# Summing the ninth chunk's first x earlier and centring it later, and moving one set of PE transposes behind eight products, in a fused linear-attention and MLP kernel

## The chip, the cores and the metric

The kernel runs on one core of one Trainium2 chip. The metric is the device time of one execution in microseconds. The engines are named as in the profile: PE (TensorE; its weight loads are PEld), DVE (VectorE, "Vector" in the text), ACT (ScalarE, "Scalar"), POOL (GpSimd) and SP (SyncE, which here only issues DMAs). Inputs are float32; the kernel computes in bfloat16 with float32 accumulation and writes float32.

## The reference

Shapes: batch B = 8, heads H = 8, sequence S = 576, head dimension D = 64, so the model width DM is 512 and the hidden width 2048.

```python
q_s = softmax(q, axis=-1)                  # over the 64 entries of a head
k_s = softmax(k, axis=2)                   # over the sequence
kv  = einsum('bhsd,bhse->bhde', k_s, v)
x   = einsum('bhsd,bhde->bhse', q_s, kv)   # then heads side by side: (B, S, 512)
xn  = (x - mean(x)) / sqrt(var(x) + 1e-6) * g_ln
out = x + relu(xn @ w_ch1) @ w_ch2
```

## The kernel before, in words

**Chunks.** The rows are worked in nine chunks of 512 rows, four tiles of 128. Chunks 1 to 8 (`c` = 0 to 7 in the code) hold the first 512 rows of each batch. The ninth (`C9` = 8) holds the 64 rows that are left of each of the eight batches. While PE runs the MLP of one chunk, the attention part of the next one is done between its matmuls; during chunk 8 this is the ninth chunk's.

**A tile's way to the MLP.** `po_mm` (L377) multiplies the exponentials of q with the batch's `kv` into a PSUM tile `po`; there are two such PSUM banks. `x_fast` (L410) does two Vector operations: L413 scales `po` by the reciprocals of q's sums (`rq`), writes x and sums it over the row by an accumulator (a second short instruction, DVE_READ_ACCUMULATOR, writes the sum into `mv`), and `xn_out` (L402, operation L405) writes `xn` = 512 x - sum, that is the centred x. `square_sum` (L395, Scalar) sums the squares of the centred x for the variance. `xn` is then transposed to `xnT`, two tiles at a time by a transposing DMA on SP (`xn_T`, L260), or, for batch 1's four tiles at the end of chunk 1, by PE: `xn_pT` (L918) calls `pe_T` (L895), four transposes into a PSUM tile `ptr` (L898) and a copy out of it, for tiles 0 and 1 by Scalar (L900).

**The MLP.** From chunk 3 on the first layer (`mm1_fast`, L718), and from chunk 2 on the second (`mm2_fast`, L649), use seven products in place of eight. In the first layer the hidden columns go in two halves, each of seven products in the order 1, 5, 6, 2, 7, 3, 4, each product of 2 groups x 4 matmuls of 256 columns. Products 1, 6, 7 and 4 accumulate onto one another in the same PSUM banks `bx` (one for each group), and between them Scalar and Vector take what they need: after product 1 a Scalar copy (`bc`), after 5 a Scalar copy (`s`), after 6 a Vector add into `bb` (L746), after 7 a Vector add that makes a quarter of `hT` (`out_22`, L749). Product 4 writes over what L749 reads, so it waits for it, group by group. Every second group's quarter then gets its relu on Vector (L754). `hs` are sums of blocks of `hT` (`sum_h`, L543), for the second layer's products.

**The order of the work** is written out by hand. `run` (L811) goes through the chunk's matmuls, each with a weight, and ahead of the matmul at which the sum of weights reaches a side task's position it issues that task. An engine's instructions run in the order of their issue. In chunk 8 a first-layer matmul counts 0.5: the second half begins at 28, product 6 ends at 40, product 7 at 48, product 4 at 56, and the second layer begins there. In chunk 1 the second layer (`mm2_stream`, L508, matmuls `pc` of 512 columns) counts 1 a matmul and goes from 64 to 128; batch 1's work at its end is in the list at L1094 to L1120.

The side tasks of chunk 8 are in `attn_rest` (L881): the ninth chunk's q sums (steps 1 and 27) and their reciprocal (28), `po` of tiles 0 and 1 (14) and of tiles 2 and 3 (58), `x_fast` at 40.5, 54, 66 and 75, `square_sum`, and the transposing DMAs at 61 and 78. `sum_h` has two more positions in chunk 8: 30 and 41.

`att_ps` has two PSUM banks (`po`, and the products `pkv` of k and v), `mm_ps` six for all else; which of the six a tile gets follows from the order in which tiles are released.

Of the kernel before, what the change touches and what calls it, by code (L numbers as in the profile page):

```python
# [20 lines left out]
def kernel(  # L21
# [16 lines left out]
    nc = tc.nc  # L38
# [14 lines left out]
    C9 = B  # L53
# [43 lines left out]
    def load_w2(k0, kn=4):  # L97
        rows = slice(k0, k0 + kn)
        nc.gpsimd.dma_start(w2_sb[:, rows, :], w2_src[:, rows, :])
# [105 lines left out]
    def reduce_q(c, t, tn=1):  # L205
        ts = slice(t, t + tn)
        nc.vector.reduce_sum(eqs[c][1][:, ts], eqs[c][0][:, ts], axis=AX.X)  # L207
# [25 lines left out]
    def sum_x(c, i):  # L233

        if i == 0:
            tqs[c] = mlp.tile([P, 4, 2, 2, P], BF16, tag="tq", name="tq", bufs=1)
        (b11, b12), (b21, b22) = [
            [xnTs[c][:, 2 * half : 2 * half + 2, 2 * kh : 2 * kh + 2, :] for half in range(2)]
            for kh in range(2)
        ]  # L240
        t1, t2, t3, t4 = [tqs[c][:, n] for n in range(4)]
        dst, x, y = ((t1, b12, b11), (t2, b22, t1), (t3, b22, b12), (t4, b21, t2))[i]
        eng = nc.vector if c >= C9 - 1 else nc.gpsimd
        for t in range(2):
            eng.tensor_tensor(out=dst[:, t], in0=x[:, t], in1=y[:, t], op=ALU.subtract)  # L245
# [6 lines left out]
    def dma_T(dst, src, t0, tn):  # L252
        nc.sync.dma_start_transpose(
            dst[:, t0 : t0 + tn].rearrange("p t j c -> p (t j) c"), src
        )
# [4 lines left out]
    def xn_T(c, t0, tn):  # L260
        dma_T(xnTs[c], xs[c][2][:, t0 : t0 + tn].rearrange("p t n -> p (t n)"), t0, tn)
# [104 lines left out]
    def start_x(c):  # L366
        xs[c] = (
            mlp.tile([P, T, DM], BF16, tag="x", name="x"),
            mlp.tile([P, T, 6], FP32, tag="st", name="st"),
            mlp.tile([P, T, DM], BF16, tag="xn", name="xn", bufs=1),  # L370
            mlp.tile([P, T, 2], FP32, tag="mv", name="mv"),
        )
        xnTs[c] = mlp.tile([P, T, KO1, P], BF16, tag="xnT", name="xnT")
# [21 lines left out]
    def square_sum(c, t):  # L395
        x, _, _, mv = xs[c]
        nc.scalar.activation(  # L397
            scrap, x[:, t], AF.Square, bias=mv[:, t, 0:1], scale=-float(DM),
            accum_out=mv[:, t, 1:2],
        )  # L400

    def xn_out(c, t, cols=slice(0, 512)):  # L402

        x, _, xn, mv = xs[c]
        nc.vector.tensor_scalar(  # L405
            out=xn[:, t, cols], in0=x[:, t, cols], scalar1=float(DM), scalar2=mv[:, t, 0:1],
            op0=ALU.mult, op1=ALU.subtract,
        )

    def x_fast(c, t):  # L410

        x, _, _, mv = xs[c]
        nc.vector.scalar_tensor_tensor(  # L413
            x[:, t].rearrange("p (h d) -> p h d", h=H),
            in0=pobox[c, t].rearrange("p (h d) -> p h d", h=H), scalar=1.0,
            in1=eqs[c][2][:, t].to_broadcast([P, H, D]), op0=ALU.mult, op1=ALU.mult,
            accum_out=mv[:, t, 0:1],
        )
        xn_out(c, t)

    def x_plain(t):

# [3 lines left out]
    def rstd_op(c):  # L426
        mv = xs[c][3]
        lnv = sml.tile([P, T], FP32, tag="lnv", name="lnv")
        rstds[c] = mlp.tile([P, T], FP32, tag="rstd", name="rstd")
        nc.scalar.activation(  # L430
            lnv, mv[:, :, 1], AF.Ln, bias=eps_ln, scale=1.0 / DM ** 3
        )
        nc.scalar.activation(rstds[c], lnv, AF.Exp, scale=-0.5)
# [373 lines left out]
    def spread(fns, a, b):  # L807
        n = len(fns)
        return [(a + (b - a) * i / n, fn) for i, fn in enumerate(fns)]
# [29 lines left out]
    def recip_q(c):  # L839
        nc.vector.reciprocal(eqs[c][2], eqs[c][1])  # L840
# [40 lines left out]
    def attn_rest():  # L881

        s = [(1, lambda: reduce_q(C9, 0, 2)), (27, lambda: reduce_q(C9, 2, 2)), (28, lambda: recip_q(C9)), (4, lambda: start_x(C9))]
        for t, (p0, p1, p2) in enumerate(((14, 40.5, 48), (14, 54, 62), (58, 66, 69), (58, 75, 77))):
            s += [(p0, lambda t=t: [po_mm(C9, t, i) for i in range(NP)])]
            s += [(p1, lambda t=t: x_fast(C9, t)), (p2, lambda t=t: square_sum(C9, t))]
        s += [(61, lambda: xn_T(C9, 0, 2)), (78, lambda: xn_T(C9, 2, 2)), (88, lambda: rstd_op(C9))]
        return s + spread([lambda i=i: sum_x(C9, i) for i in range(4)], 102, 104)

    def norm_q(b, t):  # L890
# [24 lines left out]
    def eq_pT(c, t, eng):  # L915
        pe_T(eqTs[c], eqs[c][0][:, t].rearrange("p h d -> p (h d)"), t, eng)

    def xn_pT(c, t, eng):  # L918
        pe_T(xnTs[c], xs[c][2][:, t], t, eng, None if c else g_col)
# [154 lines left out]
    with tc.manual_schedule(  # L1074
        engines={mybir.EngineType.PE, mybir.EngineType.DVE, mybir.EngineType.Activation,
                 mybir.EngineType.SP, mybir.EngineType.Pool}
    ):
        first_batch()
        load_behind(1, (2, 0))
        load_w2(8)  # L1080
        load_behind(1, (1,))
        load_w2(12, 2)
        load_w2(14, 2)
        load_behind(2)

        def po_x(c, t):
            for i in range(NP):
                po_mm(c, t, i)
            x_fast(c, t)

        run(
            mlp_steps(0),
            [
                (4, lambda: (eq_pT(0, 3, nc.scalar), x_plain(0), q0_rest(2), x_fast(0, 2))),  # L1094
                (8, lambda: (q0_rest(3), x_fast(0, 3))),
                (8.5, lambda: x_plain(1)),
                (10, lambda: xn_pT(0, 2, nc.vector)),
                (14.5, lambda: xn_pT(0, 3, nc.vector)),
                (22, lambda: square_sum(0, 0)),
                (26, lambda: square_sum(0, 1)),  # L1100
                (30, lambda: square_sum(0, 2)),
                (34, lambda: square_sum(0, 3)),
                (38, lambda: rstd_op(0)),
            ]
            + [(70, lambda: exp_q(1, 0, 4)), (72, lambda: exp_q(1, 2, 4))]
            + [(75 + t, lambda t=t: reduce_q(1, t)) for t in range(T)]
            + [((82, 86, 94, 98)[t], lambda t=t: eq_pT(1, t, nc.scalar)) for t in range(T)]
            + [(84, lambda: nc.vector.reciprocal(eqs[1][2], eqs[1][1]))]
            + [(88, lambda: exp_k(1, 0, 4)), (92, lambda: exp_k(1, 2, 4))]
            + [(26 + 4 * i, lambda i=i: scale_w1(i % KO1, i // KO1)) for i in range(2 * KO1)]  # L1110
            + [(p, lambda i=i: quarter_w2(i, 0)) for i, p in enumerate((60, 62, 64, 66))]
            + [(p, lambda i=i: sum_w1(i, 0)) for i, p in enumerate((80, 84, 88, 92))]
            + [(p, lambda i=i: sum_w1(i, 1)) for i, p in enumerate((96, 98))]
            + [(103 + 0.4 * j, lambda j=j: cast_v(1, j)) for j in range(2)]
            + [(104.5, lambda: prep_kvrem(1))]
            + [(111, lambda: (kv_all(1), start_x(1)))]
            + [(117, lambda: (po_x(1, 0), po_x(1, 1)))]
            + [(121.5, lambda: xn_pT(1, 0, nc.scalar)), (125, lambda: square_sum(1, 0))]
            + [(124.1, lambda: (po_x(1, 2), po_x(1, 3)))]
            + [(124, lambda: xn_pT(1, 1, nc.scalar)), (127, lambda: square_sum(1, 1))]  # L1120
        )
        for c in range(1, B):
            side = []
            if c == 1:
                side += second_side()
            else:
                if c + 1 < B:
                    side += attn_fast(c + 1)
                else:
                    side += attn_rest()  # L1130
                    side += [(6 + i, lambda i=i: sum_x(c, i)) for i in (2, 3)]
                if c + 2 < B:
                    side += [(1, lambda b=c + 2: load_batch(b))]
                    side += [(26, lambda b=c + 2: load_v(b))]
                    side += prep_fast(c + 2)
            if c == B - 2:
                side += [(1, load_qrem)]
                side += spread([lambda r=r: exp_qrem(r) for r in range(T)], 58, 80)
                side += [(84, lambda: eq_T(C9))]
            sums = [(57, 0)] if c == FAST else [(p, i) for i, p in enumerate((30, 41))]  # L1140
            run(mlp_steps(c), side + [(at, lambda i=i: sum_h(0, i)) for at, i in sums])
        run(mlp_steps(C9), [(33 + 3 * i, lambda i=i: sum_h(0, i)) for i in range(2)])
# [30 lines left out]
```

## Time and profile before

| what | value |
|---|---|
| median of 3 runs | 265.0 us (264.79 to 265.59) |
| profiled execution | 265.22 us |
| its span, first to last instruction | 263.0 us |
| PE busy | 257.0 us of the span (98%) |
| DVE, ACT, POOL busy | 216.8, 181.2, 77.2 us |
| granted TensorE clock | 1.00 |

A row of the instructions in order of time gives start, length, engine, line and operation, what is written from what, the count, and in brackets how long the engine had been idle and what ended this. Where a row holds several instructions ("x8"), its length goes from the first one's start to the last one's end. PE's matmuls overlap: the next one starts before the end of the one ahead of it is reached, so their pace is read from start to start. A row of the waits gives engine and line, the engine and line waited for, the total, the number of times and the longest.

### The profile page before, as it was taken

To read this page: it belongs to the slowest core of one execution; us is meant where nothing else is said; L and a number is where in the kernel's file an instruction comes from. 1 tells how busy PE (TensorE), PEld (TensorE's weight loads), DVE (VectorE), ACT (ScalarE), POOL (GpSimd) and SP (SyncE) were. 2 spreads that over 40 slices of the span, in tenths; PEclk is the share of its full clock that TensorE was granted. 3 is DMA by queue.
4 is the path that set the end of the run, shared out by engine and by line. 5 is a ranking of instruction groups with operands and counts; after the bars stand their busy time and mean duration, and the time that the engine had idled before them with its cause. 6 is when DMAs were issued, how large, how long until landed. Compare 5 with 4: busy or idle time off the path is not lost.

```text
span 263.0 us, 6811 instructions
## 1 busy us (share of the span) xinstructions
PE 257.0 (98%) x2700; PEld 218.1 (83%) x2700; DVE 216.8 (82%) x480; ACT 181.2 (69%) x356; POOL 77.2 (29%) x128
## 2 busy tenths in 40 slices
PE   8999999999999999999999999999999999999993
PEld 5799755766888998899889989998898887888883
DVE  5657686988989997899789978997899889977873
ACT  4688671997966788678867886788777477438400
POOL 8751226303067008500850095009100300030000
PEclk9999999999999999999999999999999999999999
DMA  6999999979967994899489969997807610422014
GB/s 220 258 201 206 339 213 311 277 157 287 177 125 219 300 157 81 248 285 142 79 275 277 127 76 280 266 129 152 248 3 95 188 44 0 82 87 75 0 42 120
DMA packets 69879, 45.00 MB, mean 171 GB/s; under 512 B 41492, under 2 KB 66072, under 8 KB 69848
## 3 DMA queue, kind: packets, MB, share of 16 engines
q0 software_dynamic: 20352, 22.29, 39.1%
q1 hardware_dynamic: 48896, 21.76, 38.4%
q10 hardware_dynamic: 600, 0.53, 0.6%
q8 instruction: 21, 0.34, 0.6%
q14 instruction: 10, 0.08, 0.1%
HBM read 36.70 MB, written 9.44 MB: 175 GB/s over the span
## 4 chain that ended last, share of the span: by engine, by line
PE 94%; DVE 3%; ACT 1%; issue 0%; ACTq 0%
PE ba L563 21%; PE bx L715 17%; PE bb L715 8%; PE ph L466 8%; PE bb L563 5%; PE be L563 5%; PE bc L563 5%; PE pc L512 5%; PE bc L715 5%; PE warm L829 3%; PE ph L451 3%; PE po L383 2%; PE pkv L347 2%; PE ptr L898 1%; PE xt L320 1%; DVE x L413 1%
## 5 line engine op out<-in xcount | busy, mean ns | idle before, releaser
L563 PEld LDWEIGHTS <-hs 128*128 128x128 bf16 x512 | 49.6, 98 | 5.6
L715 PEld LDWEIGHTS <-w_q 128*128 128x128 bf16 x448 | 43.2, 98 | 4.9
L563 PEld LDWEIGHTS <-hT 128*128 128x128 bf16 x392 | 37.3, 98 | 4.4
L715 PEld LDWEIGHTS <-w1g 128*128 128x128 bf16 x336 | 32.2, 98 | 4.9 <-issue 1.0
L245 POOL TENSOR_TENSOR tq<-xnT 128x256 bf16<-128x256 bf16 x20 | 12.9, 661 | 79.1 <-DMA xnT<-xn 46.7
L563 PE MATMUL ba<-w_q,hs 128*128 128x256 bf16 x256 | 31.7, 273 | 0.0
L580 POOL DMA_DIRECT2D out_dram<-ot x28 | 15.3, 555 | 47.0 <-DVE ot L574 47.0
L715 PE MATMUL bx<-tq,w_q 128*128 128x256 bf16 x224 | 29.0, 273 | 0.0
L397 ACT ACTIVATE scrap<-x,mv 128x512 bf16<-128x512 bf16 x36 | 25.9, 720 | 1.7 <-DVE x L413 1.3
L413 DVE SCALAR_TENSOR_TENSOR x<-po,rq 128x512 bf16<-128x512 f32 x34 | 23.3, 685 | 1.4 <-PE po L383 1.2
L739 ACT COPY bc<-bx 128x512 f32<-128x512 f32 x28 | 15.2, 593 | 13.0 <-PE bx L715 13.0
L746 DVE TENSOR_TENSOR bb<-bx,s 128x512 f32<-128x512 f32 x28 | 18.2, 694 | 7.1 <-ACT s L743 7.1
L757 ACT ACTIVATE hT<-bc 128x512 bf16<-128x512 f32 x28 | 15.3, 594 | 12.2 <-PE bc L715 12.2
L543 DVE TENSOR_TENSOR hs<-hT 128x1024 bf16<-128x1024 bf16 x32 | 20.9, 674 | 0.9 <-ACT hT L757 0.5
L207 DVE TENSOR_REDUCE zq<-eq 128x16 f32<-128x1024 bf16 (+1 forms) x20 | 20.8, 1051 | 1.0 <-ACT eq L190 0.8
L757 ACT ACTIVATE hT<-bb 128x512 bf16<-128x512 f32 x28 | 15.2, 594 | 8.2 <-PE bb L715 8.2
L749 DVE TENSOR_TENSOR hT<-bx,s 128x512 bf16<-128x512 f32 x28 | 18.0, 684 | 2.8 <-PE bx L715 2.8
L383 PE MATMUL po<-kv_sb,eqT 128*128 128x128 bf16 x120 | 20.2, 219 | 0.0
L588 ACT COPY s<-ba 128x512 f32<-128x512 f32 x15 | 8.7, 579 | 12.0 <-PE ba L563 7.3
L563 PE MATMUL ba<-w_sb,hT 128*128 128x256 bf16 x128 | 16.7, 273 | 0.0
L563 PE MATMUL bb<-w_q,hs 128*128 128x256 bf16 x128 | 16.5, 273 | 0.0
L757 ACT ACTIVATE hT<-bx 128x512 bf16<-128x512 f32 x28 | 15.4, 603 | 0.5 <-PE bx L715 0.5
(146 smaller groups left out, 539.3 us busy)
## 6 DMA issues: line engine op xcount, KB each, us to landing
out_dram<-ot POOLq DMA_DIRECT2D x32, 256.0 KB, 5.9
qt<-in_q_dram SPq DMA_DIRECT2D x5, 1024.0 KB, 7.2
kt<-in_k_dram SPq DMA_DIRECT2D x5, 1024.0 KB, 14.6
vt<-in_v_dram POOLq DMA_DIRECT2D x7, 512.0 KB, 14.0
qt<-in_q_dram POOLq DMA_DIRECT2D x2, 1024.0 KB, 12.6
kt<-in_k_dram POOLq DMA_DIRECT2D x2, 1024.0 KB, 13.4
w_sb<-in_moe_w_ch_dram POOLq DMA_DIRECT2D x3, 512.0 KB, 15.9
kt<-in_k_dram SPq DMA_DIRECT2D x4, 288.0 KB, 4.7
```

The source lines that it names most:

```text
L207: nc.vector.reduce_sum(eqs[c][1][:, ts], eqs[c][0][:, ts], axis=AX.X)
L383: nc.tensor.matmul(pobox["p"][:, i * P : i * P + P], eqTs[c][:, t, i, :], kv_sb[:, c, i, :], start=True, stop=True,)
L397: nc.scalar.activation(scrap, x[:, t], AF.Square, bias=mv[:, t, 0:1], scale=-float(DM), accum_out=mv[:, t, 1:2],)
L413: nc.vector.scalar_tensor_tensor(x[:, t].rearrange("p (h d) -> p h d", h=H), in0=pobox[c, t].rearrange("p (h d) -> p h d", h=H), scalar=1. ...
L466: nc.tensor.matmul(ph[:, m % 2, at : at + tn], (w1g if c else w1_sb)[:, ko, m * P : (m + 1) * P], xnTs[c][:, t0 : t0 + tn, ko, :], start=( ...
L543: nc.vector.tensor_tensor(out=dst, in0=x, in1=y, op=op)
L563: nc.tensor.matmul(dst, lhsT, rhs, start=first and (own or t == 0) and k == 0, stop=k == KH - 1, skip_group_check=True)
L580: nc.gpsimd.dma_start(out[c, 0:SM, :].rearrange("(p t) n -> p t n", t=T)[:, t], ybox[c, t])
L715: nc.tensor.matmul(dst[:, q], lhsT, rhs, start=first and q == 0 and ko == 0, stop=ko == 1, skip_group_check=True)
L746: nc.vector.tensor_tensor(out=at[g, "b"], in0=at[g, "x"], in1=at[g, "s"], op=ALU.add)
L749: nc.vector.tensor_tensor(out=h_out(g, 1, 1), in0=at[g, "x"], in1=at[g, "s"], op=ALU.add)
L757: nc.scalar.activation(h_out(g, odd, half), at[g, name], AF.Relu)
```

## The change

Two things. The ninth chunk's first tile: its L413 is issued at step 31 of chunk 8 instead of 40.5, without its `xn_out`, which is issued at 54.5, behind the second tile's `x_fast` (54); its `square_sum` moves from 48 to 46, which changes nothing in Scalar's order. And in chunk 1, `xn_pT` of batch 1's tile 1 moves from position 124 to 124.5, behind the products and x of tiles 2 and 3 (124.1). No operation is added or removed.

On Vector, the first x goes from behind the two `bb` adds of chunk 8's second half to ahead of them, and the first `xn` from there to behind the second tile's `xn`. On PE, the four transposes of tile 1 go behind one `pc` and the eight `po` matmuls of tiles 2 and 3. Since tiles are then allocated in another order, the next twelve or so tiles in `mm_ps` get other banks; from then on each tile follows the same predecessor as before. The queues of Scalar, GpSimd and SP keep their order.

```diff
-    def x_fast(c, t):
+    def x_fast(c, t, centre=True):
...
-        xn_out(c, t)
+        if centre:
+            xn_out(c, t)
...
     def attn_rest():
...
-        for t, (p0, p1, p2) in enumerate(((14, 40.5, 48), (14, 54, 62), (58, 66, 69), (58, 75, 77))):
+        for t, (p0, p1, p2) in enumerate(((14, 31, 46), (14, 54, 62), (58, 66, 69), (58, 75, 77))):
             s += [(p0, lambda t=t: [po_mm(C9, t, i) for i in range(NP)])]
-            s += [(p1, lambda t=t: x_fast(C9, t)), (p2, lambda t=t: square_sum(C9, t))]
+            s += [(p1, lambda t=t: x_fast(C9, t, t > 0)), (p2, lambda t=t: square_sum(C9, t))]
         s += [(61, lambda: xn_T(C9, 0, 2)), (78, lambda: xn_T(C9, 2, 2)), (88, lambda: rstd_op(C9))]
+        s += [(54.5, lambda: xn_out(C9, 0))]
...
             + [(117, lambda: (po_x(1, 0), po_x(1, 1)))]
             + [(121.5, lambda: xn_pT(1, 0, nc.scalar)), (125, lambda: square_sum(1, 0))]
             + [(124.1, lambda: (po_x(1, 2), po_x(1, 3)))]
-            + [(124, lambda: xn_pT(1, 1, nc.scalar)), (127, lambda: square_sum(1, 1))]
+            + [(124.5, lambda: xn_pT(1, 1, nc.scalar)), (127, lambda: square_sum(1, 1))]
```

## The prediction, made before the result was known

> **What bounds the kernel now.** I read the page first, then who waits for whom on PE, then the instructions in order of time around the two places that the change touches.
>
> ```profile
> span 263.0 us, 6811 instructions
> ...
> PE 94%; DVE 3%; ACT 1%; issue 0%; ACTq 0%
> ```
>
> ```profile
> PE bx L715 <- DVE hT L749: 0.6, 1, 0.6
> PE ptr L898 <- DVE xn L405: 0.2, 1, 0.2
> ```
>
> The first two rows are the page's: the chain that ended last runs over PE for 94% of the span, so a microsecond counts only where PE stands still. The other two are PE's waits, apart from one in the program's first microseconds, and they are the change's two places: `bx` products wait for Vector's `hT`, and transposes (`ptr`) for Vector's `xn`. Both waits are longer than their rows, because a matmul's modelled end reaches past the moment at which the next could start. I therefore count from start to start.
>
> The first place is the second half of chunk 8's first layer, Vector and then PE in order of time:
>
> ```profile
> 215.44 0.63 DVE L543 TENSOR_TENSOR hs<-hT 128x1024 bf16<-128x1024 bf16 x1
> 216.71 1.30 DVE L746 TENSOR_TENSOR bb<-bx,s 128x512 f32<-128x512 f32 x2 [0.64 <-ACT s L743]
> 217.92 0.68 DVE L413 SCALAR_TENSOR_TENSOR x<-po,rq 128x512 bf16<-128x512 f32 x1
> 218.52 0.08 DVE L413 DVE_READ_ACCUMULATOR x<-po,rq 128x1 f32 x1
> 218.64 0.35 DVE L405 TENSOR_SCALAR xn<-x,mv 128x512 bf16<-128x512 bf16 x1
> 218.91 0.69 DVE L543 TENSOR_TENSOR hs<-hs,hT 128x1024 bf16<-128x1024 bf16 x1
> 219.51 1.28 DVE L749 TENSOR_TENSOR hT<-bx,s 128x512 bf16<-128x512 f32 x2
> ...
> 221.17 0.68 DVE L413 SCALAR_TENSOR_TENSOR x<-po,rq 128x512 bf16<-128x512 f32 x1
> ...
> 222.17 0.68 DVE L543 TENSOR_TENSOR hs<-hT 128x1024 bf16<-128x1024 bf16 x1
> ```
>
> ```profile
> 216.86 1.04 PE L715 MATMUL bc<-xnT,w1g 128*128 128x256 bf16 x8
> 217.74 1.04 PE L715 MATMUL bx<-tq,w_q 128*128 128x256 bf16 x8
> 218.61 1.04 PE L715 MATMUL bb<-xnT,w_q 128*128 128x256 bf16 x8
> 220.25 1.19 PE L715 MATMUL bx<-tq,w1g 128*128 128x256 bf16 x8 [0.60 <-DVE hT L749]
> 221.28 0.60 PE L563 MATMUL ba<-w_sb,hT 128*128 128x256 bf16 x4
> 221.81 0.64 PE L390 MATMUL po<-kv_sb,eqT 128*64 128x128 bf16 x16
> 222.38 1.48 PE L563 MATMUL ba<-w_sb,hT 128*128 128x256 bf16 x12
> 223.70 0.49 PE L563 MATMUL bb<-w_q,hs 128*128 128x256 bf16 x3
> ```
>
> Eight of these matmuls take 0.87 us from start to start (216.86, 217.74, 218.61). The last `bx` products were thus due at 219.48 and came at 220.25, 0.77 late; `ba` was due another 0.87 later, at 221.12, and came at 221.28, so 0.16 more went between the two groups of four. **PE lost 0.93 us here.** The cause is Vector's order: it waits idle for 0.64 ahead of the `bb` adds, and then from 216.71 it has no gap: two adds, the sum of x (0.72 until `xn` starts), the centring `xn` (0.27 until the next start), `hs`, and only then the two `hT` adds whose sources PE is to overwrite.
>
> The second place is the end of the first chunk, PE and one row of Vector:
>
> ```profile
> 45.77 0.59 PE L512 MATMUL pc<-w_sb,hT 128*128 128x512 bf16 x2
> 46.54 0.40 PE L898 MATMUL ptr<-ident,xn 128*128 128x128 bf16 x4 [0.17 <-DVE xn L405]
> 46.77 0.38 PE L512 MATMUL pc<-w_sb,hT 128*128 128x512 bf16 x1
> 46.99 0.61 PE L383 MATMUL po<-kv_sb,eqT 128*128 128x128 bf16 x8
> 47.43 0.81 PE L512 MATMUL pc<-w_sb,hT 128*128 128x512 bf16 x3
> 48.08 1.91 PE L466 MATMUL ph<-xnT,w1g 128*128 128x256 bf16 x16
> ```
>
> ```profile
> 46.13 0.35 DVE L405 TENSOR_SCALAR xn<-x,mv 128x512 bf16<-128x512 bf16 x1
> ```
>
> A 512-column `pc` takes 0.22 from start to start (46.77 to 46.99). Two from 45.77 end at 46.21; the transposes start at 46.54, when `xn` (end 46.48) is there. **PE lost 0.33 us here.**
>
> **The change part by part.** *The ninth chunk's first x.* No operation is added or removed: L413 with its accumulator read moves ahead of the two `bb` adds, and its L405 goes behind the second tile's L405, so behind `hT`. Its inputs are old by then: the first two tiles' products ran some 5 us earlier (step 14), and the reciprocal at step 28 stands ahead of `hs` in Vector's queue. `hs` hands over 0.60 after its start (218.91 to 219.51), so x starts at 215.44 + 0.60 = 216.04. It holds Vector 0.72, as it does now until `xn` starts, so the adds start at 216.76 instead of 216.71: x fits into the idle 0.64 but for 0.05. From the adds' start the next operation comes 1.21 later (216.71 to 217.92), and it is now `hs`; 0.60 on, at 218.57, `hT` starts instead of at 219.51.
>
> Now PE. The first `bx` came 0.74 after `hT`'s start (219.51 to 220.25): that is 219.31, and PE is due at 219.48: no wait. The second four need the second `hT`, whose pair ends 1.28 after its start, 219.85, plus the same hand-over of 0.06 (first `hT` ends some 0.69 after 219.51, PE at 220.25): 219.91. They are due at 219.48 + 0.44 = 219.92: just in time. One wait upstream becomes tighter: the `bx` products of 217.74 accumulate onto what the adds read, and their second four (218.18) need the second add, 216.76 + 1.30 + 0.06 = 218.12: 0.06 to spare. So the 0.93 goes whole, or with up to 0.05 left if the accumulator read hands over more slowly to an add than to `xn`. I take **0.92**.
>
> The Trainium skill's page "VectorE: DVE Perf Modes", section "The DRAIN you can't avoid", speaks for a larger remainder: the next operation does not start until the pipe is empty. By it x and its read would hold Vector 0.68 + 0.08 = 0.76, the second `hT` would reach PE 0.03 too late, and the sum below would be 1.03 instead of 1.06. The trace has the pair of adds in 1.30, less than 2 x 0.69, so a start comes a little ahead of the previous end; I keep 0.72.
>
> What is late next: the delayed `xn` is hidden by what stands behind the second x. The second x now starts about 221.17 - 0.94 = 220.23 and frees its PSUM bank at 220.95; the fourth tile's products need that bank in the second half of the `po` block, which moves from 221.81 to 220.88, so at about 221.08: free in time by 0.13. Vector then does two centrings (0.27 more) and is at `hs` at 221.50 instead of 222.17. Vector is thus ahead by 0.67, PE by 0.93; the difference of 0.26 must be covered by slack downstream:
>
> ```profile
> 229.14 0.88 DVE L574 SCALAR_TENSOR_TENSOR ot<-bc,rstd,x 128x256 f32<-128x256 f32 x2 [0.43 <-PE bc L563]
> 229.94 0.49 DVE L245 TENSOR_TENSOR tq<-xnT 128x256 bf16<-128x256 bf16 x2
> ```
>
> The `hs` of 222.17 feeds the second eight `bb` matmuls, due 223.70 + 0.87 - 0.93 = 223.64, while it ends at 222.18. At 229.14 Vector has stood idle for 0.43, waiting for PE: that covers the 0.26. The sync queue's transposing DMAs wait for the centrings of two tiles each; the first pair is now done in the other order but 0.67 earlier, the second pair 0.67 earlier too. What they bring is read at 229.94, where Vector itself would be up to 0.26 more ahead: a short wait may arise there, on Vector alone, since these sums are for the next chunk's products.
>
> *Batch 1's tile 1.* The four transposes go behind one `pc` and the eight `po`. PE then runs on from 46.21: `pc` to 46.42, `po` to 46.87 (0.45, 46.99 to 47.43), the transposes at once, since `xn` has been there since 46.54. The bank for the second `po` tile is free: its x was summed before `xn` started at 46.13. The three `pc` end at 46.87 + 0.22 + 0.65 = 47.74, so 0.34 earlier than 48.08. But `ph` needs Scalar's copy of these transposes:
>
> ```profile
> 46.97 0.59 ACT L900 COPY xnT<-ptr 128x512 bf16<-128x512 bf16 x1 [0.41 <-PE ptr L898]
> ...
> 49.97 1.06 ACT L477 ACTIVATE hT<-ph 128x512 bf16<-128x512 f32 x2
> 50.92 0.58 ACT L900 COPY xnT<-ptr 128x512 bf16<-128x512 bf16 x1
> ```
>
> It started 0.43 after the transposes (46.54 to 46.97), so now at 47.30, and ends at 47.89: PE can go on at about 47.92. **Of 0.33, 0.16 remains**; the rest has become a wait for the copy.
>
> Behind that copy Scalar is full. Busy PE, PEld, DVE, ACT and POOL of two stretches:
>
> ```profile
> 47.00:56.00 9.00, 9.00 (x87) 7.68 (x86) 8.56 (x17) 8.97 (x16) 2.22 (x4) 1.00 1.20 246
> 56.00:62.00 6.00, 6.00 (x69) 3.05 (x68) 4.59 (x13) 4.98 (x12) 2.36 (x4) 1.00 0.60 175
> ```
>
> Scalar works 8.97 of 9.00 us and has gaps only in the second stretch. So all its work in between comes 0.33 later while PE comes 0.16 earlier, and each place where PE waits for Scalar loses 0.49 of slack. Two are tight. Behind 48.08 come 24 `ph` (0.109 each) and two sets of transposes (0.22 each), up to 51.15; in the changed program the next `ph` takes the PSUM bank that the first relu (49.97, half of 1.06) frees. That relu now ends at 50.88, and PE is there at 50.99. Eight `ph` later, at 52.02 before and 51.86 now, the first layer turns to tiles 2 and 3 and needs the copy of 50.92: it will end at 51.83 and be seen at 51.88. So 0.14 is left. After this the banks come free about a microsecond ahead of need, and Scalar's gaps take up the delay. I take **0.14**, with 0.33 as the end that no copy would limit and a loss of 0.33, Scalar's whole delay, as the other.
>
> The sum is 0.92 + 0.14 = 1.06. PE runs to the end with no other wait, so the end moves by it. The profiled execution took 265.22 us with a span of 263.0, so 2.2 lie around it: 264.16, span 261.9. That run is 0.22 above the median of 265.0; on the median's scale the forecast is **263.9**.
>
> **The rivals.** *Batch 1 gives nothing:* Scalar's delay eats the 0.14. For it: the copy's margin at 52.02 is zero. Against it: at 52.02 the copy would have to come later still. With the 0.92 alone: 264.1.
>
> *The idle time isn't usable:* x holds up the adds by its whole 0.72. Then the second `bx` four of 218.18 wait 0.61, the rest follows, and only the centring's 0.3 is gained; with batch 1's part 264.6. Against it: nothing that x reads is younger than the `hs` of 215.44.
>
> *A wait in place of the one removed (slower):* Vector starts its operations in the order of the program, as all its rows do, so if x starts at s, the adds follow at s + 0.72, and PE loses s - 216.10 at `bx` plus some 0.05 at the second `hT`. This passes the present 0.93 at s = 216.98; each 0.1 us beyond costs 0.1. It would need a late release of x's operands or of its buffer, which the seventh chunk's outputs last read. They end here:
>
> ```profile
> 207.66 0.88 DVE L574 SCALAR_TENSOR_TENSOR ot<-ba,rstd,x 128x256 f32<-128x256 f32 x2
> ```
>
> That is 208.5, far ahead. A start two microseconds late, at 218.04, without batch 1's part, gives 265.0 + 1.06 = 266.1.
>
> **How the numbers follow.** Forecast 263.9: 0.66. Batch 1 nothing, 264.1: 0.16. Idle time not usable, 264.6: 0.11. Slower, 266.1 or so: 0.07. The range reaches from 265.0 - 0.93 - 0.33 with 0.2 for the spread of a median (the three runs lie 0.8 apart), 263.5, to the third case with the same 0.2, 264.8. About 0.3%, 0.8 us, is what a measurement of this kernel can tell from no change. The forecast clears it by only 0.26, so I give a sixth of its chance and a third of the first rival's to "within": faster 0.55 + 0.11 = 0.66; within 0.28; slower by more than that 0.06.
>
> **What would show it.** The x sum at about 215.9 (all times from here about 0.15 earlier than in the rows above), the adds with hardly any idle time ahead of them, no PE wait on `hT`, chunk 8 shorter by 0.9; at the first chunk's end no wait on `xn`, a short PE wait on the copy ahead of `ph`, and the Scalar copy at 47.3. A PE wait on `bb` L746, or on Scalar between 48 and 60, would prove me wrong.

## The result, and the profile after

| | before | changed |
|---|---|---|
| median of 22 runs each | 265.44 us | 264.28 us |
| lowest and highest | 264.79, 267.15 | 263.46, 265.95 |
| ratio, 95% interval | | 0.9957 (0.9941 to 0.9973) |
| span of the profiled execution | 263.0 us | 261.9 us |

The kernel became 0.43% faster (0.27% to 0.59%), about 1.1 us. The forecast was 1.06 us, from 265.0 to 263.9; the kernel before has its median at 265.44 over 22 runs, not at the 265.0 of the first three, and that is why the time came out at 264.28 and not at 263.9.

The changed kernel's waits of PE (engine and line, what it waited for, total us, times, longest) are:

```profile
PE warm L830 <- DVE ones L960: 1.1, 1, 1.1
PE z L279 <- ACT ek L271: 0.6, 1, 0.6
```

Both waits of before, on `hT` and on `xn`, are gone. What is left lies in the first 10 us, which the change does not touch.

Chunk 8 after, Vector and then PE (line numbers are up to 2 higher than before):

```profile
215.25 0.63 DVE L544 TENSOR_TENSOR hs<-hT 128x1024 bf16<-128x1024 bf16 x1
215.80 0.68 DVE L413 SCALAR_TENSOR_TENSOR x<-po,rq 128x512 bf16<-128x512 f32 x1
...
216.52 1.30 DVE L747 TENSOR_TENSOR bb<-bx,s 128x512 f32<-128x512 f32 x2
...
218.33 1.28 DVE L750 TENSOR_TENSOR hT<-bx,s 128x512 bf16<-128x512 f32 x2
...
220.71 0.62 DVE L405 TENSOR_SCALAR xn<-x,mv 128x512 bf16<-128x512 bf16 x2
```

```profile
217.55 1.04 PE L716 MATMUL bx<-tq,w_q 128*128 128x256 bf16 x8
218.42 1.04 PE L716 MATMUL bb<-xnT,w_q 128*128 128x256 bf16 x8
219.30 1.04 PE L716 MATMUL bx<-tq,w1g 128*128 128x256 bf16 x8
220.17 0.60 PE L564 MATMUL ba<-w_sb,hT 128*128 128x256 bf16 x4
```

Everything here comes 0.19 earlier than before for reasons that lie ahead of chunk 8 (`hs` at 215.25 instead of 215.44): 0.15 of it is the second part's, and 0.04 were there before the end of chunk 1. Less that, the adds start where they did (216.71 - 0.19 = 216.52), and the bracket with the idle time of 0.64 is gone: x fills it. `hT` starts 0.99 earlier, at 218.33, and the last `bx` products start 0.88 after `bb` and end without a gap: `ba` follows 0.87 after them. From the first `bx` of chunk 8 to the first `bx` of chunk 9 it was 26.72 us (207.46 to 234.18); now it is 25.80. **The first part gave 0.92 us**, as forecast.

The end of chunk 1 after, PE and then Scalar:

```profile
45.50 0.40 PE L900 MATMUL ptr<-ident,xn 128*128 128x128 bf16 x4
...
46.38 0.61 PE L383 MATMUL po<-kv_sb,eqT 128*128 128x128 bf16 x8
46.83 0.39 PE L900 MATMUL ptr<-ident,xn 128*128 128x128 bf16 x4
47.05 0.81 PE L513 MATMUL pc<-w_sb,hT 128*128 128x512 bf16 x3
47.89 1.91 PE L467 MATMUL ph<-xnT,w1g 128*128 128x256 bf16 x16
```

```profile
47.25 0.58 ACT L902 COPY xnT<-ptr 128x512 bf16<-128x512 bf16 x1 [0.73 <-PE ptr L900]
...
51.20 0.58 ACT L902 COPY xnT<-ptr 128x512 bf16<-128x512 bf16 x1
```

The transposes follow `po` without a gap. Three `pc` from 47.05 end at 47.70; `ph` starts at 47.89, when the copy (47.25 and 0.58, so 47.83) has been seen: 0.19 of new PE wait. No row of the list of waits shows it, because the last `pc`'s modelled end reaches to 47.86; it is read from start to start. Counted from tile 0's transposes (45.54 before, 45.50 now), `ph` starts after 2.39 us instead of 2.54. **The second part gave 0.15 us**, 0.14 being forecast. Together that is 1.07, or 0.40%, inside the interval of the timing.

### The profile page after: what moved, and what is told of

It reads as the page before. It is cut to its first block, busy times and chain, and to the rows that moved or that the text cites. A ratio compares the mean times of both kernels' runs of the same rounds, so it can differ in the third digit from the quotient of the medians.

```text
span 261.9 us, 6813 instructions
## 1 busy us (share of the span) xinstructions
PE 255.9 (98%) x2700; PEld 217.5 (83%) x2700; DVE 216.8 (83%) x480; ACT 180.8 (69%) x356; POOL 77.5 (30%) x128
## 4 chain that ended last, share of the span: by engine, by line
PE 95%; DMA 2%; SPq 1%; ACT 0%; issue 0%; DVE 0%
PE ba L564 21%; PE bx L716 19%; PE bb L716 9%; PE ph L467 8%; PE bb L564 5%; PE be L564 5%; PE bc L564 5%; PE pc L513 5%; PE bc L716 5%; PE ph L452 3%; PE po L383 3%; DMA kt<-in_k_dram 2%; PE pkv L347 2%; PE ptr L900 1%; PE xt L320 1%; SPq L953 1%
## 5 line engine op out<-in xcount | busy, mean ns | idle before, releaser
L413 DVE SCALAR_TENSOR_TENSOR x<-po,rq 128x512 bf16<-128x512 f32 x34 | 23.3, 686 | 1.4 <-PE po L383 1.2
L190 ACT ACTIVATE eq<-qt 128x1024 bf16<-128x1024 f32 x14 | 14.6, 1056 | 1.7 <-DMA qt<-in_q_dram 1.7
```

What stands on the lines that cost most here:

```text
L413: nc.vector.scalar_tensor_tensor(x[:, t].rearrange("p (h d) -> p h d", h=H), in0=pobox[c, t].rearrange("p (h d) -> p h d", h=H), scalar=1. ...
```

## The experiments

The times of one kernel lie some 2 us apart, and single spans cannot be compared to 0.1 us (the last point of this chapter shows why). Single chunks can: each of the chunks 4 to 7 is 26.21 us long in all twelve traces, to 0.002 us, so a PE gap in one chunk is read from that chunk's length. "Chunk 8" is from its first `bx` to that of chunk 9, "ph" the start of the first `ph` of chunk 2 after tile 0's transposes. The ratios compare the runs and are not quotients of the medians in the table.

| run | chunk 8, us | ph, us | median of runs, us | ratio to before, 95% |
|---|---|---|---|---|
| before | 26.72 | 2.54 | 265.44 (22 runs), 265.47 (29, beside a_only to ptr_later) | |
| changed | 25.80 | 2.39 | 264.28 | 0.9957 (0.9941 to 0.9973) |
| a_only | 25.80 | as before | 264.43 | 0.9970 (0.9947 to 0.9992) |
| b_only | as before | 2.39 | 265.48 | 1.0003 (0.9980 to 1.0027) |
| between | 25.80 | 2.20 | 264.67 | 0.9975 (0.9947 to 1.0004) |
| ptr_later | as before | 2.60 | 265.01 (one run) | |
| x31_with_xn | 25.99 | as before | 266.02 (one run) | |
| xn_later_only | 26.34 | as before | 266.06 (one run) | |
| x_between_adds | 26.34 | as before | 267.17 (one run) | |
| x_behind_hT | 26.22 | as before | 264.77 (one run) | |
| a_only_again | 25.80 | as before | 264.26 (one run) | |
| xn_later_again | 26.34 | as before | 265.14 (one run) | |

The single times of x31_with_xn, xn_later_only and x_between_adds hold 1.45 to 1.69 us of PE gaps in chunk 3 (the last point of this chapter), so they say nothing of the edits.

**a_only and b_only: each part alone.** The first takes back one position of the changed kernel. The second takes back all of `attn_rest` (against the kernel before it moves this position alone, 124 to 124.5; `x_fast` keeps a `centre` that nothing sets). a_only against the changed kernel:

```diff
-            + [(124.5, lambda: xn_pT(1, 1, nc.scalar)), (127, lambda: square_sum(1, 1))]
+            + [(124, lambda: xn_pT(1, 1, nc.scalar)), (127, lambda: square_sum(1, 1))]
```

Expected of a_only:

> The ninth chunk's first x alone (summed at step 31, centred at 54.5); batch 1's transposes stay where they were. Theory: it holds the chunk-8 part, 0.92 us: no PE gap at the last bx products of chunk 8's first layer (start 0.87 after bb, not 1.64), the time 0.9 us under the kernel before, ratio about 0.9965. At the end of chunk 1 the PE gap of 0.33 ahead of tile 1's transposes is there as before. Rival (the two parts need each other, or most came from the banks that changed in chunk 2): under 0.5 us.

Expected of b_only:

> Batch 1's transposes of tile 1 alone, chunk 8 as before. Theory: 0.15 us, of which the timing can show little (ratio 0.9994, not told apart from 1), and in the trace ph starts 2.39 us after tile 0's transposes instead of 2.54, with a PE gap of 0.18 ahead of it that ends with Scalar's copy; chunk 8 has its 0.93 of PE gaps. Rival (Scalar, 0.3 later through 12 us without a gap, gives the gain back): ph starts 2.39 after, but the step to tiles 2 and 3 comes no earlier than before, ratio 1.000; it would show as PE gaps between 48 and 58 us.

PE at the place in chunk 8, a_only and then b_only:

```profile
220.21 1.04 PE L716 MATMUL bb<-xnT,w_q 128*128 128x256 bf16 x8
221.08 1.04 PE L716 MATMUL bx<-tq,w1g 128*128 128x256 bf16 x8
```

```profile
219.88 1.20 PE L716 MATMUL bx<-tq,w1g 128*128 128x256 bf16 x8 [0.60 <-DVE hT L750]
220.91 0.60 PE L564 MATMUL ba<-w_sb,hT 128*128 128x256 bf16 x4
```

The parts are independent. a_only has the 0.92 whole, `bx` 0.87 after `bb`; its timed ratio stands for 0.8 us (0.2 to 1.4). b_only has the wait on `hT` as before, 1.03 from `bx` to `ba`; its `ph` at 2.39 is kept: 64 `ph` later PE is still 0.145 ahead of the kernel before. So Scalar's lag does not give it back, as the first rival of the prediction had it. The timing alone could not have told this: its interval, 0.47% or some 1.25 us, is eight times as wide as the gain.

**between: what limits the second part.** Tile 1's transposes between the products of tiles 2 and 3, all else as in the changed kernel:

```diff
-            + [(124.1, lambda: (po_x(1, 2), po_x(1, 3)))]
-            + [(124.5, lambda: xn_pT(1, 1, nc.scalar)), (127, lambda: square_sum(1, 1))]
+            + [(124.1, lambda: po_x(1, 2)), (124.2, lambda: xn_pT(1, 1, nc.scalar)), (124.3, lambda: po_x(1, 3))]
+            + [(127, lambda: square_sum(1, 1))]
```

> Both parts, but tile 1's transposes stand between the products of tile 2 and those of tile 3 instead of behind both. Theory (Scalar's copy is what limits the second part): the transposes start 0.22 us earlier, still behind the end of xn, the copy ends before the last pc does, and ph starts 2.20 us after tile 0's transposes (2.54 before, 2.39 with the change): no gap on either side, 0.34 gained instead of 0.15, the span 0.19 shorter than with the change, ratio to the kernel before about 0.995. Rival (the limit is not the copy but PSUM banks or the order of the products): ph starts 2.35 or later.

PE in this run:

```profile
45.99 0.40 PE L900 MATMUL ptr<-ident,xn 128*128 128x128 bf16 x4
...
46.88 0.39 PE L383 MATMUL po<-kv_sb,eqT 128*128 128x128 bf16 x4
47.10 0.39 PE L900 MATMUL ptr<-ident,xn 128*128 128x128 bf16 x4
47.32 0.39 PE L383 MATMUL po<-kv_sb,eqT 128*128 128x128 bf16 x4
47.55 0.81 PE L513 MATMUL pc<-w_sb,hT 128*128 128x512 bf16 x3
48.19 1.04 PE L467 MATMUL ph<-xnT,w1g 128*128 128x256 bf16 x8
```

From 45.99 to 48.19, 2.20 us, every start follows the one ahead at PE's own pace. Four products were cover enough for `xn`, and four were then left to cover the copy. So it was the copy that took 0.19 of the 0.33. In these two stretches this version beats both kernels (0.92 + 0.34 = 1.26 us). Its profiled span, 262.2 us, is not the 0.19 shorter than the changed one's that was expected: its tile 0's transposes came 0.49 later (45.99 against 45.50), ahead of both stretches. By its timing, a ratio of 0.9975 where about 0.995 was expected, it isn't told apart from the changed kernel, nor quite from the kernel before. Its gain is thus shown in the chunks alone.

**ptr_later: one product later still.** The second part alone, at 125.5 instead of 124.5, and `square_sum(1, 0)` at 125.6 instead of 125, so that it stays behind the copy:

```diff
-            + [(121.5, lambda: xn_pT(1, 0, nc.scalar)), (125, lambda: square_sum(1, 0))]
+            + [(121.5, lambda: xn_pT(1, 0, nc.scalar)), (125.6, lambda: square_sum(1, 0))]
...
-            + [(124, lambda: xn_pT(1, 1, nc.scalar)), (127, lambda: square_sum(1, 1))]
+            + [(125.5, lambda: xn_pT(1, 1, nc.scalar)), (127, lambda: square_sum(1, 1))]
```

> Batch 1's part alone, and tile 1's transposes one 512-column product later still (tile 0's square sum kept behind the copy in Scalar's order); chunk 8 as before. Theory (each step later moves the copy and with it ph): ph starts 2.61 us after tile 0's transposes, 0.07 later than in the kernel before, and a PE gap of about 0.4 stands ahead of it. Rival (once xn is ready, further delay is free): ph starts at 2.20 to 2.39.

```profile
47.03 0.59 PE L513 MATMUL pc<-w_sb,hT 128*128 128x512 bf16 x2
47.87 0.82 PE L467 MATMUL ph<-xnT,w1g 128*128 128x256 bf16 x6 [0.24 <-ACT xnT L901]
```

PE now visibly waits for Scalar's copy, 0.41 from start to start (47.03 + 0.43 to 47.87), and `ph` comes after 2.60: the wait that was removed on one side is back on the other, larger.

**x31_with_xn and xn_later_only: which of the two moves in chunk 8 did it.** The first leaves the centring behind its sum and leaves out the position 54.5; the second keeps the position 54.5 and puts x back to 40.5 (both with tile 1's transposes at 124). The first, then the second, against the kernel before:

```diff
-        for t, (p0, p1, p2) in enumerate(((14, 40.5, 48), (14, 54, 62), (58, 66, 69), (58, 75, 77))):
+        for t, (p0, p1, p2) in enumerate(((14, 31, 46), (14, 54, 62), (58, 66, 69), (58, 75, 77))):
```

```diff
-            s += [(p1, lambda t=t: x_fast(C9, t)), (p2, lambda t=t: square_sum(C9, t))]
+            s += [(p1, lambda t=t: x_fast(C9, t, t > 0)), (p2, lambda t=t: square_sum(C9, t))]
...
+        s += [(54.5, lambda: xn_out(C9, 0))]
```

> The first x summed at step 31, but centred right behind its sum, ahead of the adds (batch 1's part left out). Theory (Vector's idle time of 0.64 holds the sum's 0.72 and no more, the rest is passed on): the adds start 0.27 later than in the changed kernel, PE waits 0.16 at the second four of the bx products that follow them and 0.04 at the second hT: 0.2 us of PE gaps in place of 0.93, a gain of 0.73. Rival (there is slack behind the adds, so the centring's place is free): no PE gap, gain 0.93.

> The first x stays behind the adds as in the kernel before; only its centring moves to 54.5 (batch 1's part left out). Theory (what stands between the adds and hT counts one to one): hT comes 0.27 earlier, the PE gaps at the last bx products are 0.50 and 0.16, 0.66 in all: a gain of 0.27. Rival (the centring was most of the trouble): gaps under 0.3.

Vector in x31_with_xn, then in xn_later_only, each from the sum of x on:

```profile
217.54 0.68 DVE L413 SCALAR_TENSOR_TENSOR x<-po,rq 128x512 bf16<-128x512 f32 x1
...
218.26 0.35 DVE L405 TENSOR_SCALAR xn<-x,mv 128x512 bf16<-128x512 bf16 x1
```

```profile
219.14 0.68 DVE L413 SCALAR_TENSOR_TENSOR x<-po,rq 128x512 bf16<-128x512 f32 x1
219.75 0.08 DVE L413 DVE_READ_ACCUMULATOR x<-po,rq 128x1 f32 x1
219.75 0.69 DVE L544 TENSOR_TENSOR hs<-hs,hT 128x1024 bf16<-128x1024 bf16 x1
220.35 1.28 DVE L750 TENSOR_TENSOR hT<-bx,s 128x512 bf16<-128x512 f32 x2
```

x31_with_xn loses 25.99 - 25.80 = 0.19 us against the changed kernel, as expected (0.2): there is no room for the centring ahead of the adds. xn_later_only loses 0.54 where 0.66 was expected: `hT` came 0.39 earlier than before, not 0.27. The rows show why. With `xn` behind it, which reads the sum, the x operation holds Vector for 0.72 (217.54 to 218.26); with an operation behind it that does not read the sum, for 0.61 (219.14 to 219.75), and the accumulator read and the next operation start together. Two other followers agree: in x_between_adds, below, an add starts 0.60 after x (219.65 to 220.25), in x_behind_hT the second x 0.61 after the first (220.24 to 220.85). Removing the centring removes its own 0.27 and 0.11 of waiting for the sum.

**x_between_adds: the sum on the path.** Position 39 instead of 31, tile 1's transposes at 124:

```diff
-        for t, (p0, p1, p2) in enumerate(((14, 31, 46), (14, 54, 62), (58, 66, 69), (58, 75, 77))):
+        for t, (p0, p1, p2) in enumerate(((14, 39, 46), (14, 54, 62), (58, 66, 69), (58, 75, 77))):
```

> The first x is summed between the two bb adds instead of ahead of them, centred at 54.5 (batch 1's part left out): the case of the prediction's second rival, that the sum holds up an add by its whole 0.72. Theory: PE waits 0.60 at the second four of the bx products that follow the adds, and then hT is in time but for 0.05: 0.65 of gaps, at another place than before, a gain of 0.28. Rival (only hT's position matters): the gap is at the last bx products.

```profile
220.07 0.60 PE L716 MATMUL bx<-tq,w_q 128*128 128x256 bf16 x4
221.00 0.60 PE L716 MATMUL bx<-tq,w_q 128*128 128x256 bf16 x4 [0.34 <-DVE bb L747]
221.43 1.04 PE L716 MATMUL bb<-xnT,w_q 128*128 128x256 bf16 x8
222.31 1.08 PE L716 MATMUL bx<-tq,w1g 128*128 128x256 bf16 x8
```

```profile
219.65 0.68 DVE L413 SCALAR_TENSOR_TENSOR x<-po,rq 128x512 bf16<-128x512 f32 x1
220.25 0.08 DVE L413 DVE_READ_ACCUMULATOR x<-po,rq 128x1 f32 x1
220.25 0.69 DVE L747 TENSOR_TENSOR bb<-bx,s 128x512 f32<-128x512 f32 x1
```

The PE rows show the wait where the theory has it, at the second four behind the adds: 0.93 from start to start where 0.44 is due, 0.49; the last `bx` then lose 0.04. In all 0.54 against 0.65, smaller by the same 0.11. The second rival's place and mechanism are real; the sum ahead of both adds does not meet it.

**x_behind_hT: out of `hT`'s way, but not in the idle time.** Position 49, its square sum at 57, tile 1's transposes at 124:

```diff
-        for t, (p0, p1, p2) in enumerate(((14, 31, 46), (14, 54, 62), (58, 66, 69), (58, 75, 77))):
+        for t, (p0, p1, p2) in enumerate(((14, 49, 57), (14, 54, 62), (58, 66, 69), (58, 75, 77))):
```

> The first x is summed behind hT (step 49, its square sum at 57), next to the second tile's, both centrings behind both sums (batch 1's part left out). So nothing stands between adds and hT, but Vector's idle time ahead of the adds is not used and two sums stand ahead of the products of tiles 3 and 4. Theory (the sums also free the two PSUM banks of po): no gap at the last bx products, but the fourth tile's products, due 0.22 into the po block, wait 0.4 to 0.55 for the second x: a gain of 0.4 to 0.5. Rival (only what stands ahead of hT counts): no gap, a gain of 0.93.

```profile
219.55 1.04 PE L716 MATMUL bx<-tq,w1g 128*128 128x256 bf16 x8
220.42 0.60 PE L564 MATMUL ba<-w_sb,hT 128*128 128x256 bf16 x4
...
221.60 0.41 PE L390 MATMUL po<-kv_sb,eqT 128*64 128x128 bf16 x8 [0.20 <-DVE x L413]
```

There is no wait on `hT`, but one on the second x, whose PSUM bank the fourth tile's products need: chunk 8 loses 0.42 against the changed kernel, where the prediction of this run had 0.4 to 0.55. Clearing `hT`'s way is not enough; the sum has to go where Vector is idle.

**a_only_again and xn_later_again: why the spans disagree.** The first profiles of a_only, x31_with_xn, xn_later_only and x_between_adds had 1.45 to 1.75 us of PE gaps in chunk 3, at places that no edit touches. Two kernels were profiled again:

> The same kernel as the run of the first x alone, once more, because its profiled execution held 1.76 us of PE gaps in chunk 3 (at 78 us, at products whose operand sums came late on GpSimd, behind a late transposing DMA), which that kernel does not touch. Theory (the DMA's landing varies from one execution to the next): without these gaps, span about 261.9 to 262.1, chunk 8 again 25.80 us long. Rival (the kernel without batch 1's part has them always): the gaps are there again and the span is 263.6.

> The same kernel as the run with the centring alone moved, once more, for the same reason: 1.7 us of PE gaps in chunk 3 in its first profiled execution. Theory (chance): no such gaps in one at least of the two repeats; chunk 8 is 26.34 us long again, with 0.38 and 0.16 of gaps at the last bx products. Rival (the program's own): the gaps in both repeats.

SP's queue in a_only and then in its repeat:

```profile
52.17 3.60 SPq L253 DMA_TRANSPOSE eqT<-eq  x1
60.69 0.40 SPq L117 DMA_DIRECT2D qt<-in_q_dram  x1
...
64.26 10.16 SPq L253 DMA_TRANSPOSE xnT<-xn  x2
```

```profile
52.46 4.69 SPq L253 DMA_TRANSPOSE eqT<-eq  x1
59.35 0.40 SPq L117 DMA_DIRECT2D qt<-in_q_dram  x1
...
64.34 8.29 SPq L253 DMA_TRANSPOSE xnT<-xn  x2
```

The repeats have no such gaps (spans 262.0 instead of 263.6, and 262.9 instead of 263.8), and their chunk 8 is 25.80 and 26.34 again. So in these two kernels the gaps are not the program's own. The other two were not profiled again, but the kernel before and x_behind_hT, whose batch 1 part is the same as theirs, have no such gaps.

## Why the prediction was right

- *What bounds the kernel.* That PE bounds the time held: each gap removed came back at the end, 1.07 in the two places, 1.06 in the profiled spans. That the spans agree so closely is luck, since two spans of a_only lie 1.6 apart.
- *The 0.93 in chunk 8.* Right as a size and in its cause. 0.92 went. The three edits that leave something on Vector's way from the end of the idle time to `hT` lost 0.19, 0.54 and 0.54 of it, according to what that was.
- *x in the idle 0.64.* Right in effect, by a term that was too large. I gave x 0.72 and a start 0.60 behind `hs`. It started 0.55 behind it (215.25 to 215.80): I had read the 0.60 from another `hs`, which lasts 0.69 and not 0.63. With nothing behind it that reads the sum, x holds Vector for 0.61. By that it would let the adds go at 216.41, and they wait another 0.11 for Scalar, whose first `s` ends at 216.49; before, it ended at 216.68, and in both kernels the adds start 0.03 behind it. In this one run the 0.72 from x to the adds could also be the sum's; it is the add of x_between_adds, which did not wait for the sum, that tells the two apart. The adds and `hT` came 0.05 earlier than I had reckoned, so the margins of 0.06 and 0.01 at the `bx` products were 0.05 wider, and no wait arose there.
- *The Trainium skill's rule on the drain* ("VectorE: DVE Perf Modes", section "The DRAIN you can't avoid"), with the pipe taken to be empty at the end of a row, would have had 0.76 for x and its read. Taken so, the trace disagrees in the direction that I took, and further than I took it: 0.61. The Trainium skill adds in the same section that a next operation which is not held starts earlier. With that the trace agrees: `hs` in xn_later_only starts 0.07 ahead of x's end (219.75 against 219.14 + 0.68). That sentence I had passed over.
- *The delayed `xn`.* Hidden, as argued: the two centrings stand together at 220.71, 0.62 for both. The idle time at 229.14 shrank from 0.43 to 0.36, as this row of the changed kernel shows; I had set aside 0.26 of it, which was too much. The short wait on Vector alone that I allowed for behind it did come: `tq` starts 0.98 after this `ot` (229.01) instead of 0.80.

```profile
228.03 0.88 DVE L575 SCALAR_TENSOR_TENSOR ot<-bc,rstd,x 128x256 f32<-128x256 f32 x2 [0.36 <-PE bc L564]
```

- *Batch 1's part.* The copy as the limit, the 0.14 and Scalar's lag of 0.33 all held: the copy of tile 2's transposes came 0.32 later (51.20 instead of 50.92, with 0.04 of earlier start), and PE had to wait 0.01 for it, not more. Moving the transposes by one place in either direction moved `ph` to 2.20 and 2.60, as the copy says.
- *The rivals.* Batch 1 gave something; x's idle time was usable; no new wait took the place of the old one in chunk 8, while one did in chunk 1, with the size forecast.
- What I overrated is the timing: with 12 runs of a version the interval was 0.45% to 0.57% wide, so for parts of 0.15 us the chunk's length in the trace is the measurement, and the timed ratio only confirms it.

## What to carry to other kernels

Where an engine is idle ahead of one operation and the critical engine waits for another one a little later, look for work between the two that was ready before the idle time, and move that work as a whole number of operations. Here what fitted was free, and what was left over came through but for the slack on the way: 0.27 of centring ahead of the adds cost 0.19, and 0.61 of x behind them cost 0.54. When a wait is removed by putting work in front of the waiting instruction, follow what that instruction feeds: the cover has to be shared between the wait ahead of it and the copy behind it. Measure such changes by the length of the stretch in the trace, with a repeat if a single span looks odd.

## What the runs showed that I had not expected

- Here a Vector operation with an accumulator costs 0.11 us less when the next one does not read the sum: 0.60 to 0.61 instead of 0.72 from start to start, with three different operations behind it.
- Batch 2's q goes through a transposing DMA issued at about 52 us, and the load of the next q and k, on the same SP queue as the next transposes, is issued 0.25 to 0.44 us behind its landing in all twelve traces. That load was issued at 57.97 us in the kernel before, 59.35 in the repeat above, 60.69 in a_only. In the last case the transposes of chunk 3's x were still being issued at 74.4, and PE stood still for 1.76 us from 77 on, in two gaps, the first of them ahead of the second row:

```profile
76.25 1.03 PE L716 MATMUL bx<-xnT,w1g 128*128 128x256 bf16 x8
78.50 1.03 PE L716 MATMUL bb<-tq,w_q 128*128 128x256 bf16 x8 [1.22 <-DVE ot L575]
```

  The row names Vector, whose `ot` came last by the profile. But `tq` is made by GpSimd, whose first sum began at 77.15 in this run and at 74.33 in the kernel before, each time 0.14 after the landing of the transposes (77.01 and 74.19); in x_between_adds the row of the same products names GpSimd's `tq`. All four profiles with this gap issued the load after 60 us, all others before 59.4. Why that DMA lands early or late stays open; it may be much of the 2 us by which the times of one kernel spread, but no run here separates that.
